# Another order table for a gated linear attention and gated MLP kernel, with fewer normalisation shifts

## The chip, the cores and the metric

The kernel runs on one core of a Trainium2 chip. The metric is the device time of one execution, in microseconds (us). TensorE is written PE, VectorE DVE, ScalarE ACT, GpSimd POOL and SyncE SP, as in the profile.

## What is computed

Four batches (B) with 768 positions (S), 8 heads (H) of 48 channels (D). The first half is a recurrence over positions, the second a gated MLP with mixing over positions:

```python
for t in range(S):
    state = alpha[:, :, t, :, None] * state + np.einsum('bhd,bhe->bhde', k[:, :, t], v[:, :, t])
    y[:, :, t] = np.einsum('bhd,bhde->bhe', q[:, :, t], state)
x = y.transpose(0, 2, 1, 3).reshape(B, S, H * D)          # 768 x 384 a batch
h = np.maximum(x @ w_in, 0.0)                             # 384 -> 1024
u, v = h[..., :512], h[..., 512:]
v_n = (v - mean(v)) / np.sqrt(var(v) + 1e-06)             # over the 512 channels
v_s = np.einsum('ts,bsd->btd', w_spatial, v_n) + b_spatial[None, :, None]
out = (u * v_s) @ w_out                                   # 512 -> 384
```

## The kernel before

The recurrence is done in chunks of 128 positions, six to a batch, 24 in all (number i); two chunks make a pair j. The first four chunks (j = 0 and 1) and chunks 6 to 9 (j = 3 and 4) are loaded and prepared as a group of four, the pair j = 2 as a pair, the rest one by one. Inside a chunk the recurrence becomes matmuls:

- `ln` (ACT): logarithm of alpha. `half`, `cum`, `cums` (PE): running sums of it, by matmuls with triangles of ones; for the groups of four, `half` is the first half of a sum and `cum` the second (lines 718, 701).
- `einv`, `eexp`, `ebc` (ACT): exponentials of minus the sums, of the sums, and of the totals.
- `kt`, `kts` (POOL or DVE, line 190): keys times the inverse decay; `qt`, `qts` (DVE): queries times the decay; `vb`, `vbs`: values cast to bf16 (line 181, or 179 on ACT). For a group of four, `pm` and `vp` bring the values into order.
- `tr`, `trk` (PE) turn keys and queries, `ev`, `evs` (ACT or DVE) copy them out of PSUM.
- `upd` (PE) makes the chunks' contributions to the state (line 795 for a group of four); `z` and `S` (DVE, POOL) carry the state on, `sb` casts it.
- `sc` (PE, line 837) makes the scores, `ms`, `m` (DVE) mask them, `y` (PE, lines 855 and 417) and `ya` (line 602) the output block of a chunk, `xe` copies it out as x transposed.

The MLP follows as soon as its chunks are there: `v` and `u` (PE, line 1006) are the two halves of `x @ w_in`, `ve` and `ue` their ReLUs (ACT line 185, DVE line 187); `bn` (DVE) the mean and variance of a tile of 128 positions, `rs` (ACT) the inverse deviation of two tiles, `nm` (DVE, line 1085) the shift, -mean * rstd, of two tiles; `vn` the normalisation of a tile, on DVE (line 1097, which subtracts the mean and multiplies, and reads no shift) or on ACT (line 1093, which does scale and bias, with the shift as the bias). `wt` and `we` turn w_spatial. `s` (PE, line 1006) is the mixing, in two parts of four and two tiles; `se` (DVE, line 1153) adds the bias, `g` (POOL or DVE, line 190) multiplies by u, `o` (PE) is the output projection, `oe` its copy out, `st` (SP) the store. `cast` brings the weights to bf16, `zeros`, `tri`, `causal`, `maskq`, `ident`, `one` make constants.

All this is recorded first as a list of operations, each with the engines that it may run on and its dependencies. Then `replay` emits them in the order of the string PLAN, written out by a planner. A word of it such as `P103@6,4,5,7:512#7:424#7` is an engine's letter (P, D, A, G for POOL, S for SP), the number of the operation in the list, the PSUM banks that it takes, and fillers: matmuls of a constant fp32 tile, of so many columns, into a bank, which are issued ahead of the operation (`warm`, line 243; their results are not used). The order of the words of one letter is the order of that engine's queue; engines wait for each other by semaphores alone. So PLAN sets each engine's order, which engine does an operation that may run on several, and which PSUM banks stand in for which.

PSUM has eight banks, each held from the matmul that writes it until its last reader. io buffers for q, k, v and alpha are three deep; a load waits on SP until the old content is used up.

Of the kernel before, what the change touches and what calls it, by code (L numbers as in the profile page):

```python
# [42 lines left out]
D2 D0 D4 D1 G9 G11 G5 G6 D3 S56 S57 S59 S58 A60 S12 S169 S170 A61 S272 S171 D8 P62@0:512#0:512#0:512#0 P66@1 P67 P63  # L43
P70@2 P71 P74@3 P75 A68 A64 D79 G82 P91@4,5 P52@6 A69 A72 A76 G7 A78 A92 A84 A65 G88 G87 A73 A77 D85 D90 D81 D93 D53
D83 D80 P103@6,4,5,7:512#7:424#7 P94@0,1 D86 D104 D89 D106 G13 P97@6,2:192#2 D98 A95 P100@3,0 D101 A96 P117@3,6:376#1
P115@4,1 A99 G107 G14 A15 A173 D102 D109 P128@0,2 D119 D118 P174@5 A116 A122 A176 P130@6,4 S16 D132 D131 S172 A135
P175@1 A129 P120@3 P54@2 G110 G105 P136@0,4 A121 A178 A55 G111 G108 P133@6 G181 A180 A134 G184 A179 D112 A177 D138
P123@7,3 P141@2 S20 G276 G277 G278 G17 G19 G18 D124 D125 P151@6 P187@7,4 P126@3 S23 S274 S273 D185 A152 A127 G186 G183
G113 G114 D182 P190@5,6 A189 A192 A142 P144@3 D137 P139@4 D188 D191 A140 G22 G21 D153 D143 P199@6,5 P196@2,7 P162@4
A280 A145 P287@0 A163 P154@1 P160@3 A279 A288 A155 D200 D201 D198 D197 D164 P193@4 A161 P156@7 A157 A165 D194 D146  # L50
P158@5 A159 G195 P202@1,2 P203 S26 A204 A147 D166 P290@4 P37@5,7 D38 P34@3,6 G24 S275 S384 S396 G25 S503 S29 D35
P207@1 D148 D208 D36 A39 A289 P205 P281@7 P40@3,5 A206 A282 A167 G10 D42 P210@2 D149 D150 D41 S385 S386 D168 D209 S398
S397 P284@5 P223@6 P219@3 P221@1 A211 A291 A224 A285 D212 A283 A220 A213 D295 D301 A286 A292 D214 D222 D215 A216
P225@6 P233@2 P217@3 P229@7 P237@0 A218 A28 D298 G297 G27 D304 G294 P226 D227 G300 G303 P43@3,5 D45 P230 P234 D231
D235 A293 A44 P46@4,6 P306@5,1 D308 P238 P49@7,3 D50 D51 A48 A47 A307 P309@2,6 P315@1,4 P312@5,7 P249@3 P250 A310 A316
A314 A296 A311 A299 D313 D317 D239 G236 D251 P338@4,1 P332@7,5 P245@0 P246 G302 G305 D333 D339 G232 P318@7,6,3,2 G240
G228 D340 D319 A507 G33 D334 D321 D247 P253@4 P330@7,1 P254 P241@5 P242 G320 A388 A400 A30 A337 A331 A32 G322 P389@0
D255 P345@7,6 D243 D324 D347 A390 P341@4 A391 P335@5 G31 G325 D394 D327 D346 G393 P401@3 A342 A336 A402 A403 P257@1
A392 S492 S387 A258 P259@4 P356@2 S399 G404 G248 G323 G326 S491 S557 P343@0,7 D405 P351@3,5 P407@1,6 A357 D328 A344
A350 A408 D353 D352 P359@2 G252 G395 P348@7 A349 P354@3 D409 S505 S494 S506 P418@6,1 P413@5,0 D358 S493 S504 S559 S547  # L60
S545 S608 S558 S548 S546 A355 A360 D415 D420 P508@7 P366@3 P410@0 P371@2 P377@1 D411 D414 A260 A509 P375@0 D419 A495
D361 A372 A561 P262@5 P496@6 G244 G329 G406 G256 A367 A376 A510 D368 G412 A497 A498 P416@0 P421@3 A422 G514 G502 G500
D378 D379 D513 G512 A417 P264@2 P267@4 A499 A362 A380 A268 D363 D501 P426@0 P423@1 P435@3 P437@6 D381 A365 A427 A424
P433@4 A434 A438 A382 D263 D436 P269@0 D364 D265 D425 D428 D383 P518@1 P369@4 A511 A270 P562@6 P373@2 A374 A429 A549
P439@7 A565 P526@0 D440 D519 P453@3 D430 D431 A432 A563 A564 D370 P449@7 P550@1 P515@2,5 A516 A551 A553 D517 A552 P454
D455 D527 D567 G566 G520 G554 G456 P441@4 P442 P445@5 D443 P450 D451 P465@6 P446 D555 D447 P530@7,4 P521@2,0 P569@1,3
D522 G448 G452 P469@5 P466 P457@2 P470 D523 D531 D532 G528 G444 D471 S620 A556 P572@7 D573 A570 P458 S622 S609 S560
A612 D467 D459 P613@4 P524@5 P533@1 A624 S610 A571 P576@7,3 P585@6,0 G574 A614 A525 D586 A615 A534 P625@5 A626 A568
G472 P535@2 A627 P461@1 S621 S611 S727 S715 S718 S623 S717 G617 D618 D578 D577 S730 S729 P473@6 G628 G575 P538@3
P581@7 A536 A616 A539 P462 S781 S716 A474 D629 P631@5,4 D587 A633 D463 D582 S728 A719 P588@3 S783 S769 S782 S770 S832  # L70
S771 A589 S784 S772 G619 G529 P579@1 A580 D632 D537 P634@7 P479@6 A630 A480 P720@5 G583 G468 D635 G636 A721 P642@3,4
P637@0,2 D540 G460 G584 P476@7 P601@6 P593@1 D643 D639 D638 A731 A723 D644 G726 G464 A602 A738 G724 P590@3 P597@6 A591
P732@0 D603 D592 A735 D477 P645@4 P640@3 A541 D542 D543 D594 A646 P485@2 A641 A785 A598 A486 D544 P650@4 P657@7 P742@6
A651 D743 D652 A733 A604 D605 D607 P488@3 P661@4 A658 A662 A734 P647@6 A489 A773 G736 P595@1 D648 D606 P482@4 D649
A483 A722 D744 P663@7 A664 D737 P599@6 P659@4 P786@3 A653 A600 P673@7 P669@0 P750@6 A596 A787 A788 P774@1 A775 A789
A776 S481 S844 S833 S834 A836 A780 S835 S845 A660 S846 D654 D655 D656 D751 D725 P674 P670 P677@6 P685@5 D671 P678
P665@0 D791 D752 D675 D779 G778 G792 D679 P796@7 P666 G790 D797 P686 G672 D687 D667 P739@6,4 P793@7,3 A848 A777 D794
P693@5 A740 A795 G680 G676 P805@0 P694 P849@7 P837@6 A838 A839 A850 A840 A851 D741 P745@3,4 P754@1,2 D695 G798 G668
D746 D806 D755 P689@5 P690 D691 D747 P681@3 P700@0 P682 P697@5 G843 D756 A698 D683 P703@4 D853 D842 D704 A701 P757@5
A758 P748@0 A749 A799 P800@6,7 D802 G841 G852 P809@3,2 P855@4,5 G807 G684 G696 G688 A856 G692 D810 P759@0 S847 P858@7  # L80
P762@3 D811 D801 P709@2 P812@6 A753 A760 P803@0 A857 D859 D761 D854 A813 A804 A763 P861@5,7 P866@4,1 S699 P712@6 D863
D868 D764 D867 D862 P825@7 A826 D827 P821@1 P817@3 P814@7 A818 A765 A815 A822 G860 P869@4 A870 S702 A713 S478 S266
S484 S490 S487 S705 S261 S475 S271 G808 P864@5 D816 P823@3 P819@1 D865 P874@4 D766 D768 A824 S714 A828 A820 A875 A767
A710 D829 P871@3 D830 D831 P887@5 P885@1 P881@4 D876 D872 D873 A877 D878 D879 P913@6 P706@2 A707 P893@3 P883@7 P897@0
A884 A886 A882 A888 P889@2 D880 P894 D895 G896 P890 P898 P905@5 P906 D891 D899 P901@2 P902 G900 P914 P909@0 P910
P917@3 D903 D892 D915 G916 D904 P926@6 P920@2 P918 S708 A927 S928 A921 S922 S711 D911 D907 D908 P923@6 G912 D919
P929@2 A930 D924 S925 S931 P935@3 D936 S937 P932@6 A933 S934 P938@3 D939 S940
"""

PAIRS = (2,)
QUADS = (0,3)
PLAIN = (0, 2)
IDLE = 16
STORE_TWO = (0, 2, 4)

# [1178 lines left out]
```

## Time and profile before

| what | value |
|---|---|
| median of 3 runs | 138.7 us (137.89 to 139.02) |
| the profiled execution | 139.19 us, of which the span from first to last instruction is 137.4 |
| PE busy, share of the span | 131.0 us, 95% |
| DVE | 120.8 us, 88% |
| ACT | 108.0 us, 79% |
| POOL | 87.2 us, 63% |
| read from memory, written | 23.60 MB, 4.72 MB |

A row of the timeline gives the start in us, the time to the end, the engine, the line of the kernel, the operation, its output and inputs, and how many of them were merged; in brackets stands the idle time ahead of it and what ended it. A row of the groups gives the number, the busy time in us, the mean of one in ns, and the idle time before them. Since a helper emits most copies and products, many groups share the lines 179 to 190 and are told apart by their tiles. PE's busy time is pipelined: a matmul of 384 columns is shown with some 0.33 us and the next one starts about 0.16 us after it.

### The profile page before, as it was taken

To read this page: it belongs to the slowest core of one execution; us is meant where nothing else is said; L and a number is where in the kernel's file an instruction comes from. 1 tells how busy PE (TensorE), PEld (TensorE's weight loads), DVE (VectorE), ACT (ScalarE), POOL (GpSimd) and SP (SyncE) were. 2 spreads that over 40 slices of the span, in tenths; PEclk is the share of its full clock that TensorE was granted. 3 is DMA by queue.
4 is the path that set the end of the run, shared out by engine and by line. 5 is a ranking of instruction groups with operands and counts; after the bars stand their busy time and mean duration, and the time that the engine had idled before them with its cause. 6 is when DMAs were issued, how large, how long until landed. Compare 5 with 4: busy or idle time off the path is not lost.

```text
span 137.4 us, 5308 instructions
## 1 busy us (share of the span) xinstructions
PE 131.0 (95%) x2122; PEld 79.2 (58%) x2122; DVE 120.8 (88%) x300; ACT 108.0 (79%) x261; POOL 87.2 (63%) x146
## 2 busy tenths in 40 slices
PE   6899998999999999999999999999999999999990
PEld 3365554564646566566657666656566765565560
DVE  6259999979999999999899999997999999974871
ACT  3476998899989889999997989999965796954041
POOL 7365899967399789972079989620799842003560
PEclk9999999999999999999999999999999999999999
DMA  3999999599989796899999797899991497101055
GB/s 83 371 371 382 341 321 347 132 374 383 366 164 261 159 218 127 163 184 192 195 190 209 143 205 147 167 194 226 190 181 23 158 390 257 66 0 57 0 203 203
DMA packets 76473, 28.66 MB, mean 209 GB/s; under 512 B 63008, under 2 KB 74912, under 8 KB 76448
## 3 DMA queue, kind: packets, MB, share of 16 engines
q1 hardware_dynamic: 76416, 28.32, 78.6%
q8 instruction: 16, 0.26, 0.8%
q14 instruction: 9, 0.07, 0.2%
q0 software_dynamic: 32, 0.00, 0.0%
HBM read 23.60 MB, written 4.72 MB: 206 GB/s over the span
## 4 chain that ended last, share of the span: by engine, by line
PE 76%; ACT 6%; DVE 6%; DMA 5%; issue 3%; POOL 2%; SPq 0%; POOLq 0%; ACTq 0%
PE bank L1006 53%; DMA kc<-in_k_dram 5%; PE bank L961 3%; PE bank L945 3%; PE bank L989 3%; PE bank L417 2%; PE bank L855 2%; PE bank L899 2%; PE bank L837 2%; PE bank L933 2%; DVE vn L1097 1%; PE bank L795 1%; PE bank L772 1%; ACT uT L185 1%; DVE w_spT L181 1%
## 5 line engine op out<-in xcount | busy, mean ns | idle before, releaser
L1006 PE MATMUL bank<-w_spT,vn 128*128 128x384 bf16 x192 | 35.8, 327 | 0.3 <-DVE vn L1097 0.3
L190 POOL TENSOR_TENSOR gT<-vs,uT 128x384 bf16<-128x384 f32 x28 | 25.7, 933 | 14.3 <-DVE vs L1153 14.1
L190 POOL TENSOR_TENSOR kt<-kc,binv 128x384 bf16<-128x384 f32 x22 | 20.3, 931 | 20.3 <-ACT binv L909 15.2
L1006 PEld LDWEIGHTS <-vn 128*128 128x128 bf16 x192 | 17.4, 98 | 11.7 <-DVE vn L1097 0.7
L1006 PE MATMUL bank<-w_in,xT 128*128 128x512 bf16 x72 | 19.1, 380 | 0.2 <-ACT xT L179 0.2
L1006 PE MATMUL bank<-xT,w_in 128*128 128x384 bf16 x96 | 18.7, 326 | 0.0
L1006 PE MATMUL bank<-w_out_sb,gT 128*128 128x384 bf16 (+1 forms) x100 | 18.4, 320 | 0.0
L1153 DVE TENSOR_TENSOR vs<-bank,bsp_bc 128x384 f32<-128x384 f32 x31 | 16.3, 550 | 2.4 <-PE bank L1006 2.3
L950 DVE TENSOR_TENSOR ptm<-bank,mask 128x512 bf16<-128x512 f32 x28 | 17.9, 683 | 0.4 <-PE bank L945 0.2
L179 ACT COPY kqT<-bank 128x512 bf16<-128x512 bf16 (+1 forms) x20 | 15.0, 792 | 3.1 <-PE bank L989 1.9
L1068 DVE BATCH_NORM_STATS2 stats<-v_sb 128x6 f32<-128x512 bf16 x24 | 16.4, 682 | 0.2
L185 ACT ACTIVATE v_sb<-bank 128x512 bf16<-128x512 f32 x20 | 11.8, 599 | 1.8 <-PE bank L1006 1.5
L185 ACT ACTIVATE uT<-bank 128x384 bf16<-128x384 f32 x27 | 12.4, 495 | 0.7 <-PE bank L1006 0.6
L1006 PEld LDWEIGHTS <-w_in 128*128 128x128 bf16 x96 | 9.0, 98 | 6.7 <-DVE ptm L950 0.3
L190 DVE TENSOR_TENSOR qt<-qc,bank 128x384 bf16<-128x384 f32 x24 | 12.6, 545 | 0.2 <-DMA qc<-in_q_dram 0.2
L1006 PEld LDWEIGHTS <-gT 128*128 128x128 bf16 x100 | 9.3, 98 | 5.8
L179 ACT CAST xT<-bank 128x384 bf16<-128x384 f32 x23 | 10.4, 482 | 1.8 <-PE bank L417 1.4
L844 DVE TENSOR_TENSOR ptm<-bank,mask 128x512 bf16<-128x512 f32 x16 | 10.4, 684 | 0.0
L1006 PEld LDWEIGHTS <-xT 128*128 128x128 bf16 x72 | 6.2, 97 | 6.2 <-ACT xT L179 1.2
L179 ACT COPY raw_w<-bank 128x384 f32<-128x384 f32 x8 | 3.8, 480 | 7.3 <-PE bank L1006 7.2
L394 DVE TENSOR_TENSOR zs<-bank,state 128x384 f32<-128x384 f32 x16 | 8.8, 549 | 0.5 <-PE bank L933 0.4
L243 PE MATMUL bank<-junk 128*128 128x512 f32 (+3 forms) x14 | 8.0, 700 | 1.1 <-DVE junk L1242 1.1
(162 smaller groups left out, 265.4 us busy)
## 6 DMA issues: line engine op xcount, KB each, us to landing
ac<-in_alpha_dram SPq DMA_DIRECT2D x14, 192.0 KB, 4.4
kc<-in_k_dram SPq DMA_DIRECT2D x14, 192.0 KB, 4.0
qc<-in_q_dram SPq DMA_DIRECT2D x14, 192.0 KB, 4.4
vc<-in_v_dram SPq DMA_DIRECT2D x14, 192.0 KB, 4.1
raw_w<-in_moe_w_spatial_dram SPq DMA_DIRECT2D x3, 768.0 KB, 8.0
out_dram<-o_sb SPq DMA_DIRECT2D x9, 192.0 KB, 2.0
ac<-in_alpha_dram SPq DMA_DIRECT2D x2, 768.0 KB, 6.8
kc<-in_k_dram SPq DMA_DIRECT2D x2, 768.0 KB, 7.6
```

The costliest lines, as they stand in the source:

```text
L179: nc.scalar.copy(out=out, in_=in_)
L185: nc.scalar.activation(out=out, in_=in_, func=AF.Relu)
L190: ENG[eng].tensor_tensor(out=out, in0=in0, in1=in1, op=ALU.mult)
L243: nc.tensor.matmul(out=banks[n][:, 0:cols].rearrange("p (a b) -> p a b", a=4), lhsT=junk, rhs=junk[:, None, 0:cols // 4].to_broadcast([128 ...
L394: lambda _: nc.vector.tensor_tensor(out=zs[i % 3], in0=tp(), in1=state[(i - 1) % 3], op=ALU.add),
L844: nc.vector.tensor_tensor(out=ptm[n2][:, ci, s], in0=banks[sl.bank].rearrange("p (hp t) -> p hp t", hp=HP), in1=mask[:, 3][:, None, :].to_ ...
L945: nc.tensor.matmul(out=pt[s][:, hp, :], lhsT=kT[rows, hp, :], rhs=qT[rows, hp, :], start=True, stop=True)
L950: nc.vector.tensor_tensor(out=ptm[n2][:, ci, s], in0=banks[sl_p[s].bank].rearrange("p (hp t) -> p hp t", hp=HP), in1=mask[:, 2][:, None, : ...
L961: nc.tensor.matmul(out=place(to, 3 * hp + (0, 1, 1, 2)[x]), lhsT=heads(vb, hp, x), rhs=ptm[n2][:, ci, x // 2, hp, :], start=(turn == 0), s ...
L1006: nc.tensor.matmul(out=ps, lhsT=lhsT, rhs=rhs, start=first and n == 0, stop=last and n == len(pairs) - 1)
L1068: nc.vector.bn_stats(out=stats[tt % 2], in_=v_sb[n2][:, tt, :])
L1153: nc.vector.tensor_tensor(out=vs[d], in0=banks[sl.bank][:, 0:TH], in1=bsp_bc[:, th, :], op=ALU.add)
```

## The change

The table PLAN is another one. The order of SP's queue (loads and stores) is the same; those of the other four engines differ from the first word on. The number of matmuls is the same but for the fillers. `nm` is now one operation for each tile, and emits nothing where the tile's normalisation is on DVE; so that this is known when it is emitted, `replay` first reads each operation's engine out of the table.

```diff
 def replay(ops, held, warm, plan):
 
+    for word in plan.split():
+        op = ops[int(re.match("[A-Z]([0-9]+)", word).group(1))]
+        op.eng = LETTERS[word[0]]
     for word in plan.split():
...
-        def nm(_):
-            for x in (tt - 1, tt):
+        for x in (tt - 1, tt):
+            def nm(_, x=x):
+                if made[("vn", b, x)].eng == "DVE":
+                    return
                 nc.vector.tensor_scalar(
                     out=shift[n2][:, x:x + 1], in0=mvs[n2][:, x, 0:1], scalar1=rstd[n2][:, x:x + 1], scalar2=-1.0,
                     op0=ALU.mult, op1=ALU.mult)
 
-        op(("nm", b, tt - 1), "DVE", nm, [("rs", b, tt - 1), ("vn", b - 2, tt - 1), ("vn", b - 2, tt)])
-        for x in (tt - 1, tt):
+            op(("nm", b, x), "DVE", nm, [("rs", b, tt - 1), ("vn", b - 2, x)])
+
             def vnf(e, x=x):
...
             op(("vn", b, x), "DVE ACT", vnf,
-               [("rs", b, tt - 1), ("nm", b, tt - 1)] + [("s", b - 2, d, th, 1) for d in range(NDS) for th in range(2)])
+               [("rs", b, tt - 1), ("nm", b, x)] + [("s", b - 2, d, th, 1) for d in range(NDS) for th in range(2)])
```

The beginnings of PE's and DVE's queues, with the operations' names in place of their numbers (fillers as their columns in brackets; the last number of `u`, `s` and `se` is the half of the positions, or the part):

```
PE before: [512 512 512] half.0.0 half.0.1 cum.0.1 cum.0.0 half.1.0 cum.1.0 half.1.1 cum.1.1 tr.k.0 bb.0
  [512 424] upd.0 tr.q.0 [192] tr.k.1 tr.q.1 [376] sc.0 pm.0 pm.2 cum.2.0 sc.2 cum.2.1 y.0 bb.1 sc.3 y.2 sc.1
  v.0.0 v.0.2 tr.k.2 y.1 tr.q.2 v.0.1 y.3 sc.2.1 sc.2.0 v.0.3 cum.4.0 u.0.0.0 u.0.3.0 upd.2 u.0.1.0 u.0.2.0 ya.2
  y.4 cum.4.1 wt.1 wt.0 v.0.4 y.5 cum.3.0 wt.2 v.0.5 cum.3.1 u.0.3.1 u.0.1.1 u.0.2.1 s.0.0.0.0 ...
PE after: [512 512 480] half.1.0 half.0.0 half.0.1 cum.1.0 cum.0.0 half.1.1 cum.0.1 cum.1.1 bb.0 [216] tr.k.0
  [512 280] upd.0 bb.1 [208] tr.q.0 tr.k.1 [72] tr.q.1 [80] pm.0 [232] sc.0 sc.2 cum.2.1 pm.2 cum.2.0 y.0 [72] sc.1
  [200] y.2 sc.3 v.0.0 v.0.2 y.1 tr.k.2 [104] tr.q.2 v.0.1 y.3 sc.2.1 sc.2.0 u.0.3.0 u.0.2.0 v.0.3 u.0.0.0 u.0.1.0
  upd.2 ya.2 cum.3.0 y.4 wt.1 wt.0 y.5 v.0.4 v.0.5 u.0.1.1 u.0.3.1 u.0.0.1 wt.2 wt.3 cum.4.0 cum.3.1 cum.4.1
  u.0.2.1 s.0.2.0.0 ...
DVE before: zeros.2 zeros.0 zeros.4 zeros.1 zeros.3 triq kt.0.0 kt.1.0 vb.1.1 vb.0.0 ev.k.0.1 be.0 qt.0.1 qt.0.0
  qt.1.0 S.0 qt.1.1 z.1 ev.k.1.0 ev.q.1.0 ev.q.1.1 z.2 ms.0.1 ms.0.0 ms.2.1 ms.2.0 z.3 ms.3.1 ms.1.0 ms.1.1 ...
DVE after: zeros.3 zeros.0 triq zeros.2 zeros.1 zeros.4 kt.1.0 kt.0.0 kt.0.1 be.0 kt.1.1 ev.k.0.0 qt.1.0 qt.0.0
  qt.0.1 S.0 qt.1.1 z.1 ev.q.0.0 ev.q.1.1 ev.k.1.1 z.2 ms.0.0 ms.0.1 ms.2.1 ms.2.0 ms.1.0 ms.1.1 z.3 ms.3.0 ...
POOL before: maskq b_sp tri ident kt.0.1 causal kt.1.1 vb.1.0 cast.w_in.1.0 S.1 ...
POOL after: b_sp tri causal maskq ident vb.0.0 vb.1.0 vb.1.1 one cast.w_in.1.0 S.1 ...
```

What the two tables give each engine over the whole run, where they differ by more than one operation or where it is spoken of below:

| operation | before | after |
|---|---|---|
| `vn` | 18 DVE, 6 ACT | 22 DVE, 2 ACT |
| `ue` | 5 DVE, 27 ACT | 10 DVE, 22 ACT |
| `ve` | 4 DVE, 20 ACT | 1 DVE, 23 ACT |
| `xe` | 1 DVE, 23 ACT | 4 DVE, 20 ACT |
| `g` | 4 DVE, 28 POOL | 7 DVE, 25 POOL |
| `kt`, groups of four and pair | 2 DVE, 8 POOL | 4 DVE, 6 POOL |
| `vb` | 2 DVE, 3 ACT, 5 POOL | 3 ACT, 7 POOL |
| `vbs` | 1 DVE, 5 ACT, 8 POOL | 1 DVE, 2 ACT, 11 POOL |
| `ev` | 9 DVE, 11 ACT | 11 DVE, 9 ACT |
| `evs` | 5 DVE, 9 ACT | 3 DVE, 11 ACT |
| `S` | 6 DVE, 14 POOL | 4 DVE, 16 POOL |
| `nm`, instructions | 24 DVE | 2 DVE |

More of the change, by code (lines that the diff above doesn't have):

```diff
@@ L48 @@
[L48 to L57, printed above, removed]
@@ L83 @@
[L83 to L87, printed above, removed]
+S56 D3 S57 D0 G11 S59 G5 D8 S58 D2 D1 A60 D4 G7 S12 A61 P70@0:512#0:512#0:480#0 P62@1 P66@2 P71 G9 P63 A72 P74@3 S171
```

75 lines of the change are left out of this document (45 added, 30 removed).

## Prediction

> **What bounds the kernel now.** I read the page first (engine shares, the 40 slices), then busy time by stretch, the chain that ended last, and the timelines of TensorE, VectorE and ScalarE up to 42 us.
>
> ```profile
> span 137.4 us, 5308 instructions
> PE 131.0 (95%) x2122; PEld 79.2 (58%) x2122; DVE 120.8 (88%) x300; ACT 108.0 (79%) x261; POOL 87.2 (63%) x146
> PEclk9999999999999999999999999999999999999999
> ...
> 10.00:40.00 30.00, 28.48 (x565) 15.92 (x564) 28.53 (x67) 26.94 (x66) 23.33 (x37) 1.00 1.00 319
> 40.00:120.00 80.00, 79.95 (x1416) 50.66 (x1416) 77.14 (x175) 70.76 (x176) 52.98 (x71) 1.00 0.83 185
> 120.00:134.20 14.20, 14.18 (x90) 8.42 (x88) 10.05 (x22) 5.16 (x13) 5.28 (x20) 1.00 0.19 69
> ...
> 117.12 11.80 PE bank L1006 x70
> ...
> 134.22 0.36 DVE raw_w L181
> ```
>
> The columns of the stretches are PE, weight loads, DVE, ACT, POOL, clock, DMA share, GB/s. From 40 us to the last matmul PE is busy for 79.95 of 80.00 and 14.18 of 14.20 us, and the chain there is matmul after matmul. What is multiplied does not change, so these 94 us can't shrink; they can only be reached sooner or be broken by new waits. After the last matmul come a copy of 0.36 us and a store, to 137.4: a tail of 3.2 us that ends in the same piece (the second half of the last output tile, copied by DVE) in both tables.
>
> What can move lies before 42 us. There PE does filler and waits:
>
> ```profile
> 1.05 4.67 PE L243 MATMUL bank<-junk 128*128 128x512 f32 x6 [1.05 <-DVE junk L1242]
> 6.24 0.32 PE L718 MATMUL bank<-la,le_quad 128*128 128x384 bf16 x1 [0.52 <-ACT la L683]
> ...
> 10.05 1.84 PE L243 MATMUL bank<-junk 128*128 128x512 f32 x4
> 11.82 0.26 PE L795 MATMUL bank<-o_sb,kt 32*128 32x96 bf16 x8
> 12.33 0.78 PE L795 MATMUL bank<-o_sb,kt 32*128 32x96 bf16 x56 [0.24 <-POOL o_sb L181]
> ...
> 13.38 0.59 PE L243 MATMUL bank<-junk 128*128 128x192 f32 x2
> 13.90 0.41 PE L772 MATMUL bank<-ident,kt 64*128 64x64 bf16 x16
> ...
> 14.61 0.90 PE L243 MATMUL bank<-junk 128*128 128x376 f32 x2
> 15.44 0.40 PE L837 MATMUL bank<-kqT 48*128 48x128 bf16 x8
> ...
> 18.82 0.41 PE L855 MATMUL bank<-ptm,vb 128*32 128x128 bf16 x16
> ...
> 22.69 0.82 PE L1006 MATMUL bank<-w_in,xT 128*128 128x512 bf16 x3 [0.25 <-ACT xT L179]
> ...
> 24.14 0.40 PE L855 MATMUL bank<-ptm,vb 128*32 128x128 bf16 x14 [0.47 <-issue]
> ...
> 28.93 0.73 PE L602 MATMUL bank<-ptm,vb 64*32 64x128 bf16 x64
> ...
> 35.00 1.46 PE L1006 MATMUL bank<-w_spT,vn 128*128 128x384 bf16 x8
> ...
> 38.54 0.50 PE L1006 MATMUL bank<-w_spT,vn 128*128 128x384 bf16 x2 [0.29 <-DVE vn L1097]
> ...
> 41.81 0.41 PE L772 MATMUL bank<-ident,kt 64*128 64x64 bf16 x16
> ```
>
> Real work starts at 6.24, when ScalarE has the first logarithms; the load of alpha and SyncE's order, which sets it, are the same in both tables. From there to 40 us the fillers take (next start less own start) 1.77 + 0.52 + 0.83 = 3.12 us, and PE's idle time between 10 and 40 us is 30.00 - 28.48 = 1.52 us. DVE is idle for only 1.47 us of the same 30: this stage is bound by DVE as much as by PE.
>
> **The change, part by part.** *The normalisation shifts.* Only an ACT normalisation reads them. In the new table 2 of the 24 tiles are normalised on ACT, so 22 shifts go. The rows of the DVE groups:
>
> ```profile
> L1085 DVE TENSOR_SCALAR shift<-mvs,rstd 128x1 f32<-128x1 f32 x24 | 3.9, 206 | 1.0 <-ACT rstd L1079 1.0
> L1097 DVE TENSOR_SCALAR vn<-v_sb,mvs,rstd 128x512 bf16<-128x512 bf16 x18 | 7.6, 443 | 0.0
> L187 DVE TENSOR_SCALAR uT<-bank 128x384 bf16<-128x384 f32 x5 | 2.8, 554 | 0.2 <-PE bank L1006 0.2
> L187 DVE TENSOR_SCALAR v_sb<-bank 128x512 bf16<-128x512 f32 x4 | 2.7, 673 | 0.0
> L190 DVE TENSOR_TENSOR gT<-vs,uT 128x384 bf16<-128x384 f32 x3 | 2.2, 732 | 0.0
> L1093 ACT ACTIVATE vn<-v_sb,shift,rstd 128x512 bf16<-128x512 bf16 x6 | 4.9, 817 | 0.2 <-DVE shift L1085 0.2
> ```
>
> They free 22/24 of 3.9 = 3.6 us of DVE. The new table spends it again: 4 more normalisations (4 x 443 ns = 1.8), 5 more ReLUs of u (2.8), 3 gating products (2.2), 2 more key products (1.6, at 816 ns, row below), less 3 ReLUs of v (-2.0); the other exchanges (copies, carries) nearly cancel. 6.4 less 3.6 is about 2.8 us more at most; since instructions overlap their neighbour by some 0.08 us (14 more of them) I take +1 to +1.5 us over the whole run. ACT loses 4 x 817 ns and the ReLUs: some 4 to 5 us, on the engine that has room. So the shifts are worth nothing to the end by themselves: they only pay for the moves. If the table had not taken the moves, they could have given at most those 3.6 us, and only where DVE bounds.
>
> *The lead-in fillers* are 512, 512 and 480 columns instead of three of 512. The last ended 0.52 us ahead of the first real matmul, which waited for ACT, so the 32 columns cost or give nothing. The trace shows six passes in 4.67 us, 0.78 each, against 0.44 (1.77 over four) at 10 us, with 512 and 424 columns: TensorE is slow at first, though the clock row shows 9 throughout. Filling starts at the same instant in both tables, so that stays.
>
> *The later fillers.* Before: 512, 424, 192, 376 columns, 3.12 us. After: 216, 512, 280, 208, 72, 80, 232, 72, 200, 104. From 0.52 us for 192 and 0.83 for 376 a filler costs about 0.20 us and 1.7 ns a column (and 0.97 for the 512, its share of 512 in 936 columns in the 1.77): 0.56 + 0.97 + 0.67 + 0.55 + 0.32 + 0.33 + 0.59 + 0.32 + 0.54 + 0.37 = 5.2 us, so +2.1 us of filler. Each stands in PE's order, so it runs whether or not PE has to wait there. Its cost is between 0 (it stands in a wait) and +2.1 us.
>
> *The order up to 42 us.* I followed the new order by hand; more rows for that:
>
> ```profile
> 7.50 0.87 ACT L741 ACTIVATE binv<-bank 128x384 bf16<-128x384 f32 x2 [0.57 <-PE bank L718]
> ...
> 8.40 1.55 DVE L190 TENSOR_TENSOR kt<-kc,binv 128x384 bf16<-128x384 f32 x2 [3.59 <-ACT binv L741]
> 10.61 0.41 DVE L181 COPY kqT<-bank 128x512 bf16<-128x512 bf16 x1
> 10.94 0.54 DVE L181 CAST bsp_bc<-bank 128x384 bf16<-128x384 f32 x1
> 11.69 1.48 DVE L190 TENSOR_TENSOR qt<-qc,bank 128x384 bf16<-128x384 f32 x3 [0.20 <-DMA qc<-in_q_dram]
> 13.14 0.56 DVE L190 TENSOR_TENSOR state<-bank,bcq 128x384 f32<-128x384 f32 x1
> ...
> 1.01 1.36 POOL L339 TENSOR_SCALAR_AFFINE_SELECT mask<-mask 32x128 bf16<-32x128 bf16 x4
> ...
> 8.07 0.91 POOL L190 TENSOR_TENSOR kt<-kc,binv 128x384 bf16<-128x384 f32 x1 [3.31 <-ACT binv L741]
> 8.94 1.90 POOL L355 TENSOR_SCALAR_AFFINE_SELECT mask<-mask 64x128 bf16<-64x128 bf16 x4
> ```
>
> The first finished sum is now the fourth group, not the third, so ACT's first inverse starts about 0.25 us after 7.50. All four key products of the first super-chunk are now on DVE: from 8.3, four at 0.64 (below), the bias copy and one eviction (about 0.47 and 0.33 after overlap) give 11.7, three query products 13.1. POOL now makes its two masks (1.36 and 1.90) and the identity one after the other, behind a wait for DVE's clearing; by the walk the identity is there near 9.5, still ahead of the first transposes at about 10.2. The state update stands behind fillers of 512 and 280 columns and starts near 12.2 instead of 12.33, so the first carry is at 13.1, as before. Then the small fillers hold PE back: first scores at 16.4 instead of 15.44, second output block at 19.8 instead of 18.82. But DVE, which bounds here, does the same masks at nearly the same instants, and the waits of before at 22.69 and 24.14 go: the fourth output block starts at 24.0, where before had most of it at 24.14: level. From there the new order asks for less that is late: the block behind four u projections (L602) starts at 28.1 with 0.33 us of sums put off, against 28.93 (0.5 ahead); the first mixing matmul at 35.1 with 0.7 us more done (0.6 ahead); the last group of transposes would start at 40.6 against 41.81, 1.2 us ahead.
>
> Such a walk has no small waits in it. Before had 1.5 us of visible ones in 30 us; the new order will have about as many of its own as I could not see, so I keep 0.5 of the 1.2 us.
>
> *The stretch behind.* It needs DVE 77.14 of 80 us. DVE has 2.9 us of room there; about 1 us more work and a PE that is 0.5 us early use half of it. I take no new wait, and no gain.
>
> *Where a rule speaks against it.*
>
> ```profile
> L190 DVE TENSOR_TENSOR kt<-kc,binv x2: 636/816/995, 8.4 to 9.3; 128x384 bf16<-128x384 f32 x2
> ```
>
> The first of DVE's two key products ran beside POOL's own (8.07 to 8.98), took 995 ns and let the second start 0.92 us after it; the second, beside the mask, took 636. The Trainium skill, "SBUF — State Buffer", section "Who interferes with whom", says that a VectorE instruction with two SBUF inputs waits for a GpSimd instruction that reads SBUF, for its whole length. By that rule all four could go at 0.92 beside masks and casts, 1.1 us later, and the span would be 138.0 in place of 136.9. The 636 ns beside a mask that reads and writes SBUF does not bear out a full wait, so I sum with 0.64 and leave the other as a rival.
>
> *Sum.* 137.4 - 0.5 = 136.9 us of span. The profiled execution took 139.19 us for 137.4 of span, and stands 0.5 above the median of 138.7; the same -0.5 on the median gives 138.2 us.
>
> **The rivals.** *Fillers where PE was ready (slower).* The new fillers are 5.2 us and the old waits that they could stand in 1.5. If none of the added 2.1 us covers a wait, and nothing of the lead comes, it is 138.7 + 2.1 = 140.8 us. For: the walk has PE 1.0 us late at the second output block, just behind six small fillers. Against: DVE is the later one there, in the walk. It decides (over 1%, 1.4 us) when less than 0.7 of the added 2.1 us stands in waits.
>
> *The whole lead comes (faster).* 1.2 us of the walk, and DVE's lighter stretches let the mixing start with no wait (0.29 at 38.54 and a part of the hidden ones): 138.7 - 1.9 = 136.8. For: ACT is 4 to 5 us lighter. Against: DVE isn't, and it is at 95%.
>
> *DVE falls behind at the start.* Key products at 0.92 each: +1.1 us at the first carry, which everything up to the fourth output block follows; with the 0.5 kept, 138.7 + 1.1 - 0.5 = 139.3. For: the first product's 0.92. Against: 0.64, and the filler ahead of the update gives 0.5 us of room.
>
> *Nothing that reaches the end.* The order is another list of equal worth: 138.7.
>
> **How the numbers follow.** The forecast 0.40 at 138.2; no effect 0.12; DVE behind 0.13; fillers 0.20; whole lead 0.15. Within 1% (about what a measurement of this kernel can tell from no change) are the first three, 0.65, less a tail to each side of 0.04 and 0.05: faster 0.19, same 0.56, slower 0.25. The range reaches to the whole lead and to the filler case, 136.7 to 140.8 us; the forecast's own is 137.2 to 139.2.
>
> **What would show it.** Right: 2 shifts on DVE; the first carry near 13.1; PE without idle time from about 41 us; the last matmul at about 133.7. Filler case: fillers of 5 us and PE idle time of over 1 us between them before 25 us, scores at 16.4 or later, the mixing matmuls after 36. DVE case: the four key products at over 0.8 us each. It is wrong as a whole if PE shows waits behind 42 us, which I priced at nothing.

## The result, and the profile after

The change made the kernel slower: a median of 140.17 us (139.89 to 141.17, nine runs) against 139.02 us (137.89 to 139.84, nine runs), a ratio of 1.0104 with a 95% interval of 1.006 to 1.0147. The forecast was 138.2 us, within 136.7 to 140.8. The sign was wrong; the time is inside the range, near its upper end.

The profiled execution took 140.66 us, 1.47 more than the profiled one of before. The head of its page, and its chain:

```profile
span 138.8 us, 5294 instructions
...
PE 131.9 (95%) x2120; PEld 80.6 (58%) x2134; DVE 119.9 (86%) x288; ACT 104.2 (75%) x249; POOL 86.1 (62%) x148
...
PE 74%; DVE 12%; ACT 9%; issue 2%
```

DVE's share of the chain was 6% before, ACT's 6%, PE's 76%. The same stretches as before (PE, weight loads, DVE, ACT, POOL, clock, DMA share, GB/s):

```profile
10.00:40.00 30.00, 28.88 (x585) 17.38 (x588) 27.43 (x63) 26.26 (x64) 22.07 (x34) 1.00 0.99 319
40.00:120.00 80.00, 79.35 (x1405) 50.07 (x1414) 76.37 (x164) 67.40 (x166) 53.27 (x74) 1.00 0.78 167
120.00:134.80 14.80, 14.74 (x94) 8.72 (x91) 10.78 (x24) 5.33 (x14) 5.09 (x20) 1.00 0.43 157
```

From 10 to 40 us PE looks busier than before (28.88 against 28.48 us), but it is the added filler that fills it; DVE, which the forecast took to bound that stage as much as PE, is busy for 1.1 us less (27.43 against 28.53). Between 40 and 120 us PE now has 0.65 us of gaps, where it had 0.05.

At the end, DVE's last copy, and SyncE's last stores:

```profile
134.77 0.36 DVE L185 COPY raw_w<-bank 128x192 f32<-128x192 f32 x1 [0.62 <-PE bank L1010]
```

```profile
132.02 1.81 SPq L1201 DMA_DIRECT2D out_dram<-o_sb  x3
133.97 1.82 SPq L1201 DMA_DIRECT2D out_dram<-raw_w  x4
```

The copy starts 0.55 us later than before's 134.22. The span's 1.35 us more (138.77 against 137.42, from the unrounded records) are thus 0.55 us until then and 0.80 behind it: from the end of that copy to the end of the span it is 3.64 us, and was 2.84. The missing 0.12 of the 1.47 us lies outside the span.

**How far PE is at which time.** Fillers hide how late the work is, and the two tables have other orders. So I went through each trace's weight loads in PE's order, left the fillers out, and added up the time that the matmuls take at the pace that they have in before's later part. The table gives the instant (us) at which so much work was behind PE; e2, e9, e12 and e17 are runs told below (e12 is before with a delay at 51 us, the starred values stand behind it):

```
work done   before   e12      after    e2       e9       e17
   9 us     19.81    19.89    21.20    21.04    20.98    21.18
  22        35.66    34.94    36.24    35.75    35.92    35.94
  36        51.70    50.51    51.76    51.27    51.44    51.46
  45        60.48    60.11*   61.49    60.99    61.16    61.17
  80        95.14    94.75*   95.56    95.25    95.23    95.24
 118       133.22   132.83*  133.78   133.56   133.45   133.44
```

Two things are to be seen. Between 36 and 45 us of work every kernel with the new table takes 9.72 us, and before 8.78: 0.94 more, of which some 0.6 come back by 80. And at 36 the profiled executions of before and after seem level, at 51.7; but e12, whose order is before's and which has had nothing done to it by then, is 1.2 us ahead of both. Where before's profiled execution lost them shows beside e12, on PE at 24 us, before first, then e12:

```profile
23.44 0.23 PE L855 MATMUL bank<-ptm,vb 128*32 128x128 bf16 x2
24.14 0.40 PE L855 MATMUL bank<-ptm,vb 128*32 128x128 bf16 x14 [0.47 <-issue]
```

```profile
23.52 0.41 PE L857 MATMUL bank<-ptm,vb 128*32 128x128 bf16 x16
23.75 0.34 PE L419 MATMUL bank<-kqT,sbd 128*32 128x128 bf16 x12
```

The same block runs through in e12, and in e7 (told below), which has before's words up to 109 us and the same PE rows as e12 from 7 to 41 us, to 0.01 us. The wait of 0.47 us, and one of 0.29 at 38.54 which both lack too, belong to this execution and not to the order. The transposes that start at 41.81 in before start at 40.62 in e12 and e7. In the runs beside e17 before's spans lie at 136.1 to 136.5 (six) or at 136.9 to 137.5 (five); beside the other experiments they fill that range without a gap. The profiled one, 137.4, is near its upper end. So at 36 us of work the new start is 0.8 (e2) to 1.25 us (after's own execution) behind the best executions of the old one; the middle loses some 0.5 net, and the tail 0.3 to 0.8 in the profiles.

What such a wait may be shows from where it stands. The twenty profiles have twelve waits of PE between 8 and 60 us that are named "issue", are longer than 0.13 us and end at an instruction that waits for no semaphore. Eleven of them stand behind a multiple of 256 and 191 to 193 more of PE's instructions (matmuls and weight loads, fillers with them), counted from the first, and these eleven end 1.3 to 1.5 us behind the end of a fetch of 16 KB on q8, a queue whose kind in the trace is instruction. Among them are the 0.47 us above, 0.22 at 17.96 and 0.15 at 24.16 in after, and 0.77 at 23.88 in e11. So PE most likely waits there for its own instructions, which come late in some executions of an order and not in others. No run was made to change it.

### The profile page after: what moved, and what is told of

Same layout as the page of the kernel before. It is cut to its first block, busy times and chain, and to the rows that moved or that the text cites. A ratio compares the mean times of both kernels' runs of the same rounds, so it can differ in the third digit from the quotient of the medians.

```text
span 138.8 us, 5294 instructions
## 1 busy us (share of the span) xinstructions
PE 131.9 (95%) x2120; PEld 80.6 (58%) x2134; DVE 119.9 (86%) x288; ACT 104.2 (75%) x249; POOL 86.1 (62%) x148
## 4 chain that ended last, share of the span: by engine, by line
PE 74%; DVE 12%; ACT 9%; issue 2%
PE bank L1010 44%; PE bank L247 8%; DVE stats L1072 3%; PE bank L965 2%; PE bank L949 2%; PE bank L722 2%; PE bank L993 2%; DVE ptm L591 2%; PE bank L776 2%; PE bank L841 2%; ACT uT L189 2%; PE bank L421 2%; PE bank L903 1%; ACT v_sb L189 1%; PE bank L859 1%
## 5 line engine op out<-in xcount | busy, mean ns | idle before, releaser
L194 POOL TENSOR_TENSOR kt<-kc,binv 128x384 bf16<-128x384 f32 x20 | 18.3, 924 | 20.9 <-ACT binv L913 13.9
L194 POOL TENSOR_TENSOR gT<-vs,uT 128x384 bf16<-128x384 f32 x25 | 22.5, 915 | 13.2 <-DVE vs L1159 13.1
L1159 DVE TENSOR_TENSOR vs<-bank,bsp_bc 128x384 f32<-128x384 f32 x31 | 16.4, 550 | 3.0 <-PE bank L1010 1.9
L1010 PE MATMUL bank<-w_in,xT 128*128 128x512 bf16 x58 | 17.5, 379 | 1.0 <-issue 0.3
L183 ACT COPY kqT<-bank 128x1024 bf16<-128x1024 bf16 (+1 forms) x20 | 16.1, 822 | 2.3 <-PE bank L993 1.1
L189 ACT ACTIVATE uT<-bank 128x384 bf16<-128x384 f32 x22 | 10.2, 493 | 6.7 <-PE bank L1010 6.5
L189 ACT ACTIVATE v_sb<-bank 128x512 bf16<-128x512 f32 x23 | 13.6, 598 | 1.4 <-PE bank L1010 1.3
L183 ACT CAST xT<-bank 128x384 bf16<-128x384 f32 x20 | 9.5, 490 | 3.9 <-PE bank L421 3.0
L247 PE MATMUL bank<-junk 128*128 128x512 f32 (+9 forms) x26 | 11.1, 537 | 1.1 <-DVE junk L1248 1.1
L913 ACT ACTIVATE binv<-bank 128x384 bf16<-128x384 f32 x14 | 6.7, 495 | 2.7 <-PE bank L903 2.6
```

Source lines behind the costliest of these rows:

```text
L183: nc.scalar.copy(out=out, in_=in_)
L189: nc.scalar.activation(out=out, in_=in_, func=AF.Relu)
L194: ENG[eng].tensor_tensor(out=out, in0=in0, in1=in1, op=ALU.mult)
L247: nc.tensor.matmul(out=banks[n][:, 0:cols].rearrange("p (a b) -> p a b", a=4), lhsT=junk, rhs=junk[:, None, 0:cols // 4].to_broadcast([128 ...
L913: op(("einvs", i), "ACT", lambda _: nc.scalar.activation(out=buf, in_=sums(), func=AF.Exp, scale=-1.0), [("cums", i)] + readers("kt", j - ...
L1010: nc.tensor.matmul(out=ps, lhsT=lhsT, rhs=rhs, start=first and n == 0, stop=last and n == len(pairs) - 1)
```

## The experiments

The rivals were: the fillers; the order of the start; the middle; the stores at the end. Each ratio is to before, run on the same chip.

**The fillers: e1 and e3.** After and before, each without the fillers behind the first real matmul.

```diff
-P91@5,6:216#5 ... P103@5,6,4,7:512#7:280#7 ... P94@2,1:208#1 ... P117@3,1:232#2
+P91@5,6 ... P103@5,6,4,7 ... P94@2,1 ... P117@3,1
...
-P123@6,2:72#6 ... P133@5:200#3 ... P192@4,0:104#5
+P123@6,2 ... P133@5 ... P192@4,0
```

> The new table without the ten fillers behind the first real matmul (the three of the lead-in stay). Filler theory: the fillers take 5.3 us of TensorE's time, 2.2 more than before's, and stand partly where TensorE was ready or hold back scores for which VectorE waits; without them the first mixing matmul comes about 1 us sooner, the time falls by 0.8 to 1.5 us, from 140.2 to about 139, and TensorE's idle time before 40 us rises by only some 4 us. Order theory: the fillers stand in waits that the order makes anyway (VectorE, PSUM banks); then idle time replaces them one for one and the time stays within 0.4 us of 140.2.

> The table of before without its four later fillers (512, 424, 192 and 376 columns). If fillers cost where they stand, it is faster than before, by up to 1 us of their 3.1; if they stand in waits, it stays at 139.0 within 0.3 us; if they keep TensorE's clock up, the matmuls from 10 us on are slower and the time rises.

Measured: e1 140.56 us, ratio 1.0162 (1.0118 to 1.0205). e3 142.32 us; no ratio is formed for it, since its executions lie apart with the clock: the one with a mean granted clock of 0.999 took 139.69 us, the five at 0.952 to 0.964 took 141.96 to 143.17. The clock rows of e1 and then e3 (40 slices of 3.5 us):

```profile
PEclk9996558999999999999999999999999999999999
```

```profile
PEclk9999555999999999999999999999999999999999
```

So the fillers hold the clock: without them it falls to half for some 10 us, and before loses 3.7 us by it in the median. After without them is no faster, and PE has done 11 us of work at 24.34 in e1 and at 24.37 in after. But e1 changes two things at once: the fillers' 5.4 us go, and real work runs at half the clock in their place (PE is busy for 4.00 of the 4 us from 18 to 22 at a granted 0.52). The two can cancel. So e1 doesn't show that the fillers cost nothing, and their rival stands; e11 bears on it below. That the clock falls needs no long idle time. e3's PE in the stretch ahead, and its longest wait in it:

```profile
10.00:14.00 4.00, 1.79 (x92) 1.21 (x84) 3.80 (x10) 2.90 (x9) 2.43 (x6) 1.00 1.09 379
14.00:18.00 4.00, 3.45 (x67) 1.96 (x67) 3.65 (x8) 3.84 (x9) 3.39 (x6) 0.52 1.12 340
```

```profile
11.82 0.27 PE L795 MATMUL bank<-o_sb,kt 32*128 32x96 bf16 x8 [1.41 <-DVE bsp_bc L181]
```

PE was busy for 1.79 of 4 us, never idle for more than 1.41 in one piece, and the granted clock was 0.52 behind that. The Trainium skill, "TensorE: Matmul & The Clock Gate", section "What's actually happening", has the clock fall after an idle window of some 3.4 us, and rise again after as much busy time. The trace agrees with the halving; that the window must be idle it does not bear out, since half busy was enough.

**The shifts alone: e4.** Before's table on the new code, so that 18 of 24 shifts go and no engine's order changes.

```diff
-PLAN = the new table
+PLAN = the old table, in the new numbers (one nm word for each tile)
```

> The table of before, with the new code for the shifts alone: 18 of 24 shift instructions of 0.2 us go from VectorE's queue, 3 us in all. If VectorE's load bounds the end, it gains 0.5 us or more; by my account it is TensorE that bounds behind 42 us, so no more than 0.3 us, 138.7 to 139.0.

Measured: 138.61 us, ratio 0.9995 (0.997 to 1.002). The shifts are worth nothing by themselves in the time. (The tail of e4's profile is 0.36 us longer than before's, for a reason that stands under e13 to e18, and its last copy ends 0.30 sooner; a gain of that size could hide there.)

**The stores: e2.** ScalarE's copy `oe.17` stands behind three ReLUs of the last batch, so in after the stores of tiles 17 and 15 leave at 130.4 us only, in one crowd with the last ones. Here it is moved ahead of them.

```diff
-(oe.17 behind ue.3.1.1, ue.3.0.1 and ue.3.3.1 on ACT)
+(oe.17 right behind vn.3.5)
```

> The new table with one word moved on ScalarE: the copy of output tile 17 ahead of the three ReLUs of u that it stood behind, so that the stores 17 and 15 leave near 125 us, not at 130.4. Store theory: they are 384 KB that fall into the drain of the end; without them the stretch from the last copy to the end of the span is 3.2 us again in place of 4.0, and the time falls by about 0.8 us, to 139.4. Rival: the tail is set by the last store alone, and the time stays at 140.2 within 0.3 us.

Measured: 140.27 us, ratio 1.0131 (1.0094 to 1.0169). The two stores leave at 123.31, and nothing is gained: the tail still is 3.31 us.

**Splices: e5 to e8.** One table up to a word, then the other's remaining words in their order: the start of before with the rest of after (e5, to the first mixing), the reverse (e6), and the same at about 109 us (e7 ends as after, e8 as before).

```diff
-PLAN = the new table
+PLAN = one table's words up to s.0.0.0.0 (e5), s.0.2.0.0 (e6), v.3.0 (e7, e8), then the words left over of the other
```

> The words of before up to its first mixing matmul (about 35 us), then the words of the new table in their order. Head theory (the new start loses the time, VectorE idling for scores that come late): 138.7, the time of before. Rest theory (the new order behind 35 us loses it, by ScalarE's waits from 53 to 67 us and by the end): 140, the time of the new table.

> The reverse: the words of the new table up to its first mixing matmul, then those of before. Head theory: 140. Rest theory: 138.7. If both of these come out between, each part has its share.

> The words of before up to the first v projection of the last batch (about 109 us), then those of the new table. End theory: in the new table tile 16's output projection, its copy and the stores of tiles 15 to 17 fall into the last 8 us, and the stretch behind the last matmul is 3.6 to 4.0 us against 3.2; then this is 0.5 to 0.9 us slower than before, 139.2 to 139.6. Rival: the end only passes on a delay from ahead of it, and this is 138.7.

> The words of the new table up to the first v projection of the last batch, then those of before. End theory: 139.2 to 139.5, the delay of about 0.5 us from ahead of it without the long tail. Rival: 140.

Measured: 1.0162 (1.0118 to 1.0206), 1.026 (1.0222 to 1.0298), 1.0268 (1.0218 to 1.0317) and 1.0187 (1.0148 to 1.0226). All medians are above those of both parents (e5's interval reaches after's), so the times can't say which half is at fault. The traces say it for the middle. Reckoned once more, with the mean intervals between weight loads as the pace, the stretch from 36 to 45 us of work takes 8.63 to 8.66 us in before, e3, e4, e6, e7 and e10, which all have before's words there. It takes 9.39 to 9.45 in after and in the twelve other runs that have after's words there, e5 among them. So the 0.8 to 0.9 us belong to these words, whatever start or end goes with them. The seam itself costs: PE in e7 around it,

```profile
104.00:108.00 4.00, 4.00 (x100) 2.77 (x98) 3.98 (x9) 1.85 (x6) 3.37 (x4) 1.00 0.21 73
108.00:112.00 4.00, 2.00 (x51) 1.07 (x47) 2.34 (x5) 3.02 (x5) 2.72 (x5) 1.00 1.06 392
```

stands for 2 of 4 us. A table's rest counts on the state that its own start leaves.

**What a late engine costs: e10 and e12.** Before, with ten small fills on DVE ahead of `z.3`, or with four small copies on ACT ahead of `vp.8`.

```diff
+        if op.key == ('z', 3):        # e12: ('vp', 8)
+            delay()                   # 10 x nc.vector.memset(pad, 0.0); e12: 4 x nc.scalar.copy(out=pad, in_=pad)
         op.emit(eng)
```

> Before with ten small fills of a spare tile on DVE ahead of z.3, some 1.5 us there at 18 to 20 us, and nothing else: the reverse of the mending. Theory (DVE is the bound from there to the first mixing, and what it loses lasts to the end): 0.6 to 1.5 over before. Rival (the start has room, a late DVE is caught up before 52 us): within 0.3 of before.

> Before with four small copies on ScalarE ahead of vp.8, about 1 us there at 52 us, where the change's PE falls 0.5 us behind in its profile and catches up by 80 us. Theory (a loss on ScalarE in the middle is made up where TensorE's stretch has room): within 0.3 of before. Rival (it lasts): 0.6 to 1.0 over before.

The delays as they came out, in e10 and in e12:

```profile
19.12 2.49 DVE L1250 MEMSET pad<- 128x128 f32 x10
```

```profile
51.03 1.28 ACT L1250 COPY pad<-pad 128x128 f32<-128x128 f32 x4
```

Measured: e10 1.0156 (1.0095 to 1.0218) for a delay of 2.5 us, not the 1.5 meant; PE stood idle for 2.28 us, and the granted clock from 22 to 26 us was 0.61; two of its runs with a mean clock of 1.00 took 140.2 and 140.3 us, so some 1.8 us come without the clock. e12 1.0054 (1.0018 to 1.0089), 0.75 us for 1.3 us of ACT; in the table above it takes 9.60 us where before takes 8.78, and makes nothing of it good by the end (72.72 us from 45 to 118, before 72.74). So a delay of DVE at 20 us, or of ACT at 52 us, lasts. My expectation that the middle would make it up was wrong.

**The start: e9 and e11.** In after, DVE stands idle in the middle of the masks. DVE and PE there:

```profile
16.65 2.48 DVE L848 TENSOR_TENSOR ptm<-bank,mask 128x512 bf16<-128x512 f32 x4 [0.34 <-PE bank L841]
20.26 1.29 DVE L848 TENSOR_TENSOR ptm<-bank,mask 128x512 bf16<-128x512 f32 x2 [1.13 <-ACT binv L500]
...
22.53 1.01 DVE L194 TENSOR_TENSOR qt<-qc,bank 128x384 bf16<-128x384 f32 x2
```

```profile
17.96 0.32 PE L819 MATMUL bank<-o_sb,ident 32*32 32x384 bf16 x1 [0.22 <-issue]
18.21 0.34 PE L471 MATMUL bank<-la,le_pair 128*128 128x384 bf16 x1
...
18.64 0.41 PE L859 MATMUL bank<-ptm,vb 128*32 128x128 bf16 x16
18.98 0.44 PE L247 MATMUL bank<-junk 128*128 128x72 f32 x2
19.35 0.40 PE L841 MATMUL bank<-kqT 48*128 48x128 bf16 x8
```

The first row is the masks of two chunks; they end at 19.13. The next mask needs the scores `sc.1`, which PE (last row) has only at 19.35 and after, behind an output block and a filler, and in a bank that the mask before has just given up (`P123@6,2`; bank 2 was that of `sc.2`). The releaser named, an ACT exponential, ended at 19.97. The mask doesn't read it: in the kernel's list it depends on the scores, on old output blocks and on a constant, and in e9 the masks run on across the end of that exponential, 20.44. Why the mask starts 0.5 us behind the end of the scores, 19.75, stays open. In e9 the scores get bank 7 in place of 2, without the 72 columns, ahead of the output block, and DVE's `z.3`, which frees bank 7, goes ahead of the masks of `sc.2`. e11 also drops the fillers of 232 and 200 columns and has e2's copy.

```diff
-... D132 A129 P120@1 ... D131 P123@6,2:72#6 ... D125 A134 P141@6 A182 D112
+... D112 D132 A129 P123@6,7 P120@1 ... D131 ... D125 A134 P141@6 A182
```

> After's table with the second scores (sc.1) given banks 6 and 7 in place of 6 and 2 and set ahead of the first output block on PE (without their 72 filling columns), and DVE's z.3, which frees bank 7, set ahead of the masks of the third scores. Theory (the start is bound by DVE, and it loses 1.13 us at 19.13 because sc.1 waits for the bank that DVE's own mask ms.2.0 frees): the idle time of 1.13 us goes, the masks, z.3 and the second pair's query products are done at 23.0 to 23.3 in place of 24.14, the first mixing starts at 35.3 to 35.9, and the median is 0.5 to 0.9 under after's 140.2. Rival (what the start loses is given back by 52 us, since the profiles of before and after stand level there): the first mixing is earlier but the median stays within 0.3 of 140.2. Rival (fillers ahead of PE's ready work): no change in the start either, since only 72 columns go.

> The kernel of e9_after_sc1_banks with the fillers ahead of the first scores (232 columns) and of the third output block (200) taken out, and ScalarE's copy oe.17 moved behind vn.3.5 as in e2. Theory of the start: another 0.3 us of DVE's idle time at 16.3 goes, the median is 139.0 to 139.6. Rival of the clock: with fewer fillers the granted clock falls to half between 10 and 20 us as in e1 and the start loses what it gained; 139.8 to 140.5. Rival that the start doesn't count: within 0.3 of 140.2.

Measured: e9 1.0156 (1.0107 to 1.0206), e11 1.0124 (1.0079 to 1.0169), its clock at 1.00: no gain that six runs can tell. Yet in e9 the idle time is gone, and another has come:

```profile
18.66 3.08 DVE L848 TENSOR_TENSOR ptm<-bank,mask 128x512 bf16<-128x512 f32 x5
21.99 1.02 DVE L194 TENSOR_TENSOR qt<-qc,bank 128x384 bf16<-128x384 f32 x2 [0.26 <-ACT bank L503]
22.93 0.68 DVE L848 TENSOR_TENSOR ptm<-bank,mask 128x512 bf16<-128x512 f32 x1
24.14 1.08 DVE L185 COPY kqT<-bank 128x512 bf16<-128x512 bf16 x3 [0.53 <-PE bank L540]
```

Five masks in a row, then a wait for ACT's exponential (L503), and one for PE. The exponential is late as well. Its rows on ACT, in before (L496, L499) and in after (L500, L503):

```profile
16.93 0.52 ACT L496 ACTIVATE binv<-bank 128x384 bf16<-128x384 f32 x1
...
20.28 0.87 ACT L499 ACTIVATE bank<-bank 128x384 f32<-128x384 f32 x2
```

```profile
17.41 0.49 ACT L500 ACTIVATE binv<-bank 128x384 bf16<-128x384 f32 x1 [0.35 <-PE bank L476]
...
19.47 0.50 ACT L500 ACTIVATE binv<-bank 128x384 bf16<-128x384 f32 x1
...
20.84 0.48 ACT L183 CAST xT<-bank 128x384 bf16<-128x384 f32 x1 [0.49 <-PE bank L421]
...
21.60 0.47 ACT L503 ACTIVATE bank<-bank 128x384 f32<-128x384 f32 x1
```

The last exponential of the pair ends at 21.15 in before, 22.07 in after and 21.95 in e9. In after ACT does it behind the copy of the second output block, for which it waits for 0.49 us; PE has that block at 20.21 to 20.79, behind a filler of 200 columns. So the late scores and the late exponential both lead back to PE's queue. The chain of after's page does too:

```profile
19.05 0.37 PE bank L247 x2
19.42 0.33 PE bank L841 x8
19.75 0.54 PE bank L247 x2
20.28 0.34 PE bank L859 x16
...
24.16 0.31 PE bank L540 x7
24.47 1.08 DVE kqT L185 x3
```

From 4.83 to 24.47 us it is PE's, with less than 0.5 us of waits in it and with all ten fillers (L247), 5.4 us; from there to the first mixing it is DVE's almost throughout. Without their fillers PE would have to wait at some of these places, so not all of the 5.4 us are a cost. e11 has 232 and 200 columns less than e9, at the full clock, and its third output block (L859) starts at 21.46 against 22.23. The 0.77 us of PE's late instructions at 23.88 then take this lead, and the first mixing starts at 35.86, against 35.90. So e11's profile can't tell what these fillers cost in the end, and its median, 0.45 us under e9's, lies within the noise. Whether the start loses by fillers where PE was ready or by the order itself is not settled.

**The tail: e13 to e18.** The queue of the trace that is named instruction carries fetches of 8 KB. In after one begins 0.55 us behind DVE's last copy, in before the last two begin 3 us ahead of it. The last 5 us of after, in 40 slices of 0.125 us, then of before:

```profile
DMA  7999999999999997599999600010000000000000
...
q14 instruction: 1, 0.01, 1.2%
```

```profile
DMA  8189999999999999999994299999920000000000
```

In before all DMA engines end together. In after most end at slice 23, and single packets trail on for some 0.8 us. The six runs pad one queue each, or two, to shift that fetch: DVE's by 16 small fills at the start (e13), ACT's by 16 small copies there (e14), both (e15, e16 with e9's mending), POOL's by 30 fills ahead of `g.3.1.0` (e17), SyncE's by 16 loads of four bytes ahead of `st.12` (e18).

```diff
+    for _ in range(15): nc.vector.memset(pad, 0.0)        # e13, e15, e16, behind a first one
+    for _ in range(16): nc.scalar.copy(out=pad, in_=pad)  # e14, e15, e16
...
+        if op.key == ('g', 3, 1, 0):                      # e17
+            for _ in range(30): nc.gpsimd.memset(idle, 0.0)
...
+        if op.key == ('st', 12):                          # e18
+            for x in range(16): nc.sync.dma_start(out=small[x], in_=moe_b_spatial[None, 0:1])
```

> After with 16 more small fills of a spare tile on DVE at the very start, where it waits for data anyway. Theory (the fetch of instructions in the last microseconds is DVE's, which now has 12 instructions fewer): the fetch that comes at 135.6 comes at some 125 to 132 us, the time from the last copy to the end falls from 3.64 to 2.8 to 2.9, and the median is 0.3 to 0.7 under after's 140.2. Rival (ACT's fetch): the fetch and the tail stay, and nothing changes. Rival (chance): the fetch moves and the tail stays over 3.1.

> After with 16 more small copies of a spare tile on ACT at the very start, ahead of its first logarithm (it is idle there from 2.0 to 5.3 us), and one small fill on DVE. Theory (the fetch is ACT's, which now has 12 instructions fewer): fetch at some 125 to 132 us, tail 2.8 to 2.9, median 0.3 to 0.7 under after's 140.2. Rival (DVE's fetch): fetch and tail stay. Rival (chance): the fetch moves and the tail stays over 3.1.

> After with both paddings, 16 on DVE and 16 on ACT at the start. Theory of the fetch: whosever it is, it comes before 132 us, the tail is 2.8 to 2.9, the median 0.3 to 0.7 under after's 140.2 (139.5 to 139.9). Rival (chance, or another engine's fetch): tail over 3.1, median within 0.3 of 140.2.

> The kernel of e9_after_sc1_banks (the second scores with banks of their own) with both paddings. If the tail's 0.5 to 0.8 goes, 139.0 to 139.9, still over before by what the start and the middle lose on TensorE (the last weight load at 134.1 against before's 133.5 to 133.9). Rival: 140.1 to 140.6 as e9.

> After with 30 more small fills of a spare tile on GpSimd ahead of its product g.3.1.0 (batch 3, slice 1), some 4.6 us in the 10.25 us for which it stands idle before 126.4. Theory (the fetch 0.5 us after the last copy is GpSimd's, and it is what holds up the last store): the fetch moves to 132 us or earlier, the time from the last copy to the end is 2.8 to 2.9 in place of 3.64, the median 0.3 to 0.7 under after's 140.2. Rival (SyncE's fetch): fetch and tail stay, nothing changes. Rival (chance): the fetch moves and the tail stays over 3.1.

> After with 16 more loads of four bytes on SyncE's queue ahead of the store st.12, in its idle time between 101 and 112 us. Theory (the fetch is SyncE's): the fetch moves to 132 us or earlier, the tail is 2.8 to 2.9, the median 0.3 to 0.7 under after's 140.2. Rival (GpSimd's): fetch and tail stay, nothing changes. Rival (chance): the fetch moves and the tail stays over 3.1.

Measured: e13 1.0168 (1.0122 to 1.0215), e14 1.0176 (1.0142 to 1.021), e15 1.0179 (1.0148 to 1.0211), e16 1.0176 (1.0144 to 1.0207): the paddings delay the start (1 us of work is done at 7.71, 7.28, 8.10 and 8.11 us, after 7.04; profiles without them reach 7.6) and leave the fetch where it is. e17 1.0109 (1.0059 to 1.0159), 139.69 us, and e18 1.011 (1.0064 to 1.0157), 139.77 us. In e17 the fetch moved to 118 us, and the last 5 us look like before's:

```profile
115.73 5.24 POOL L1253 MEMSET idle<- 128x1 f32 x30
```

```profile
DMA  9993007999899999999992699999700000000000
```

Its tail is 2.87 us. All profiles, from the end of the last copy (us), with the fetch that falls between 0.2 us ahead of it and 1 us behind:

```
no fetch there     before 2.84  e3 2.83  e5 2.92  e7 2.91  e10 2.85  e12 2.83  e17 2.87
fetch, its length  e6 0.31: 3.61   e9 0.33: 3.14   e4 0.42: 3.20   e1 0.43: 3.12   e18 0.47: 3.16
                   e15 0.59: 3.42  e11 0.60: 3.27  e13 0.60: 3.29  e2 0.64: 3.31
                   e16 0.67: 3.53  e14 0.76: 3.63  e8 0.77: 3.54   after 0.93: 3.64
```

So the fetch is POOL's, and in the profiles it is what holds up the last store: by 0.3 us at the least and 0.8 in after's. In the times this is not shown. e17's median is 0.5 us under after's, as foretold, but before's beside it is lower too (138.26 against 139.02), and its ratio, 1.0109, is no better than after's 1.0104. e17 and e18 differ in the tail by 0.29 us in the profiles, and in the median by 0.08, less than six runs can tell. e4 has the fetch there and before's time. No kernel here beats before.

## Why the prediction was wrong

*The shifts* (nothing by themselves, paid out for moves): right in the time, e4 at 0.9995. Two are left, as foretold, and DVE has 119.9 us of work in place of 120.8. Its sum of +1 to +1.5 us for DVE was off by about 2 us, without weight here.

*The fillers* (between nothing and +2.1 us): not settled. The rival of fillers where PE was ready gave the time best, 140.8, and after's chain runs through all ten of them up to 24.47 us. Of its signs two came (fillers of 5 us, here 5.4, and the mixing after 36) and two did not (scores at 16.4 or later, idle time of over 1 us between the fillers). e1 can't refute it, since the clock fell, and e11 shows 0.77 us of it up to 22 us and nothing behind.

*The key products*: the four took 0.55 to 0.83 us each, the first carry came at 13.05 (forecast 13.1). The rival, and the rule of the Trainium skill, "SBUF — State Buffer", section "Who interferes with whom", that stood beside it, are not borne out: POOL was at casts and masks then, and even the slowest, at 10.20 beside a cast, shows no full wait.

*The order up to 42 us*: this step failed. It was right as far as the first scores (16.14, forecast 16.4) and wrong from there: second output block 20.21 (19.8), fourth 25.12 (24.0), the block that before has on L602 29.34 (28.1), and the first mixing here:

```profile
36.22 1.95 PE L1010 MATMUL bank<-w_spT,vn 128*128 128x384 bf16 x11
```

The forecast was 35.1. The walk had PE 1.0 us late at the second output block and let that pass, since it took DVE to be the later one there. In the run PE was the later one: DVE stood idle for 1.13 us for the scores, the chain up to 24.47 is PE's, and the 1.1 us were not made up by the mixing. That much is read from rows. What makes PE late, the fillers or the order of its queue, is not settled: e9 takes DVE's idle time away and gains nothing, since PE's queue is as long as before. And the gain of the walk was in part the end of before's waits at 22.69 and 24.14; the second is not in before's order but in one execution of it (e12 and e7 lack it). "I keep 0.5 of the 1.2 us" had the wrong sign: the start loses 0.8 to 1.25 us against the best executions of before, and gains nothing even on the profiled one. e10 shows that such a loss lasts.

*The stretch behind* (no new wait, no gain): failed by some 0.5 us net. Between 52 and 61 us the new words cost 0.94 us, the same in four profiles and, by e5 and e6, whatever the start. Why is read from rows alone: the chain there is ACT's, where before's is PE's:

```profile
53.72 0.88 ACT vb L183 x2
54.60 0.34 ACT kqT L183
54.94 0.42 issue
55.37 0.51 ACT v_sb L189
55.87 0.47 ACT xT L183
```

That ACT's total went down by 4 us did not help: what counts is what it does at that moment. e12 shows that 1.3 us more of ACT there cost nearly as much; which of its operations it is was not tried.

*The tail* (the same piece in both tables, so the same 3.2 us): failed in the profiles, by 0.3 to 0.8 us. The piece is the same, but POOL's fetch of instructions falls beside its store.

The sum then is 0.8 to 1.25 us at the start, 0.5 behind it and 0.3 to 0.8 at the end: 1.6 to 2.55 us against the best executions of before. After's profile has the larger figure of each, and stands 1.35 us of span over before's, which had lost 1.2 us of its own. That the time still lies inside the range is luck in part: the upper end stood for the fillers, which are not settled, and what the middle and the tail lose was in no rival. What the forecast said would refute it, waits of PE behind 42 us, is what came: 0.65 us of gaps where 0.05 were.

## What to carry to other kernels

Where an order is written out, ask of each idle stretch which queue it leads back to: mending the wait that you see gives nothing while that queue stays as long. A run without the fillers is also a run at a lower clock, and can't price them; take out a few, and look at the clock. Compare a forecast with more than one execution of the kernel before, since a wait in a profile may be that execution's own, and its end no gain. A table is one piece: half of it, joined to another's, was no faster than either, though the traces of such halves still tell which words cost what.

## What the hardware showed

A fetch of instructions of one engine shares the DMA engines with the data, and where it falls beside the last store the tail of the profile is 0.3 to 0.8 us longer; 30 small fills in POOL's idle time moved it by 17 us. How many instructions lie between two such fetches, and why before's table has it at 131 us, was not settled. The granted clock falls to half after 4 us in which PE was busy for 1.79, with no idle time over 1.41 us, and stays there for some 10 us. Waits of PE of up to 0.77 us stand at places that are whole multiples of 256 of its instructions apart, 1.3 to 1.5 us behind fetches of 16 KB, in some executions of an order and not in others; that PE waits there for its instructions is inferred.
